# A codec kernel on one core: 16 rows per partition, tap sums in two buffers, PSUM by single banks, and a planner with new latencies and ranks that picks the engine of each residual update

## The chip, the cores and the metric

One core of one Trainium2 chip. The metric is the device time of one execution in microseconds (us). Most executions of a kernel agree within 0.3%.

Engines: TensorE (PE) multiplies matrices into PSUM; VectorE (DVE) and ScalarE (ACT) do elementwise work and read PSUM; GpSimd (POOL) does setup fills, edge copies and the issue of output stores. A "residual update" below is one correction of a block of 128 channels by a chosen codebook row.

## The reference, cut to what matters

```python
B, T, D, K = 2, 16000, 512, 3;  Nq, C = 4, 8          # bf16
xp = pad(x, 1)                                        # on the time axis
z = silu(sum(xp[:, i:i+T] * dw_enc[i] for i in range(K)))   # depthwise taps
res, q = z, 0
for s in range(Nq):                                   # four codebooks of 8 rows
    d2 = |res|^2 - 2 res.cb[s] + |cb[s]|^2
    sel = cb[s][argmin(d2)]
    q, res = q + sel, res - sel
y = sum(pad(q, 1)[:, i:i+T] * dw_dec[i] for i in range(K))
```

## The kernel before

The time axis is cut into tiles of `G` rows on each of 128 partitions (20 tiles of 6, 8 or 14 rows). Channels then lie on the partitions, by transposing loads. Per tile: three taps and their sum (DVE), exp and reciprocal (ACT), the gate product (DVE), scores of three codebooks at once (PE, read by DVE), a chain of some 25 tiny DVE instructions that decides three codebooks in turn, 24 residual updates, a fourth score and decision, and the output rows (PE, then ACT, then a store).

Nothing is issued in program order. Each instruction is a *step* with an estimated cost; a planner written in Python simulates the engines and emits the steps of each engine in the order in which it believes they become ready. That order is then fixed. What the planner believes of a step that depends on another is this:

```python
LATENCY = {"PE": 0.26, "ACT": 0.2, "DVE": 0.13, "POOL": 0.25, "SP": 0.1, "DMA": 0.05}
...
for u in users[n]:          # steps that depend on step n, which ends at t + c
    lat = self.LATENCY[s["e"]] if steps[u]["e"] != s["e"] else s["tail"]
    at[u] = max(at[u], t + c + (s["tail"] if steps[u]["e"] != s["e"] else 0.0) + lat)
```

A dependent step on *another* engine waits 0.13 to 0.26 us. A dependent step on the *same* engine is ready at once (`tail` is 0 for compute).

The tap sums and the residual updates:

```python
for c in range(2):                                    # two blocks of 128 channels
    for k, (dst, tok) in enumerate((p0[:, c], p1[:, c], P2[i % NP2])):   # cut
        add("DVE", ts, ..., tap(dst, i, k), ...)
        if k:
            tt(p0[:, c], p0[:, c], src, ALU.add, ...)
...
ON_DVE = (3, 7, 11, 15, 19, 23)                       # of the 24 updates of a tile
on_act = m not in ON_DVE
# ACT: two matmuls (identity * z + codebook), then a copy PSUM -> z
# DVE: one matmul (codebook), then z = z + PSUM
```

Of the kernel before, what the change touches and what calls it, by code (L numbers as in the profile page):

```python
# [16 lines left out]
class Plan:  # L17



    QUOTA = 2
    LATENCY = {"PE": 0.26, "ACT": 0.2, "DVE": 0.13, "POOL": 0.25, "SP": 0.1, "DMA": 0.05}

    def __init__(self, slots):
        self.steps, self.writer, self.readers = [], {}, {}
        self.slots = slots

    def add(self, engine, cost, key, fn, reads=(), writes=(), take=None, free=None, hold=None, tail=0.0, after=(), dest=None):
        n = len(self.steps)
        deps = set(after)  # L30
        for t in reads:
            if t in self.writer:
                deps.add(self.writer[t])
            self.readers.setdefault(t, []).append(n)
        for t in writes:
            if t in self.writer:
                deps.add(self.writer[t])
            deps.update(self.readers.get(t, ()))
            self.writer[t] = n
            self.readers[t] = []  # L40
        deps.discard(n)
        self.steps.append({"n": n, "e": engine, "c": cost, "k": key, "fn": fn, "deps": deps, "take": take, "free": free,
                           "hold": hold, "tail": tail, "dest": dest})
        return n

    def order(self):
        steps = self.steps
        left = [len(s["deps"]) for s in steps]
        users = [[] for _ in steps]
# [4 lines left out]
        clock = {s["e"]: 0.0 for s in steps}  # L54
        open_ = {e: [] for e in clock}
        table = [None]
        slots = {k: [0.0] * n for k, n in self.slots.items()}
        for s in steps:
            if not left[s["n"]]:
                open_[s["e"]].append(s["n"])  # L60
        out = []
        self.busy = {e: 0.0 for e in clock}
        held = {e: 0 for e in clock}

        def ready(n):
            s = steps[n]
            t = at[n]
            if s["take"]:
                if s["dest"] and held[s["dest"]] >= self.QUOTA:
                    return float("inf")  # L70
                t = max(t, min(slots[s["take"][0]]))
            return t

        while len(out) < len(steps):
            best = None
            for e, names in open_.items():
                now = clock[e]
                pick = None
                for n in names:
                    t = max(ready(n), now)  # L80
                    if t == float("inf"):
                        continue
                    r = (t, steps[n]["k"], n)
                    if pick is None or r < pick:
                        pick = r
                if pick and (best is None or pick < best):
                    best = pick
            t, _, n = best
            s = steps[n]
            c = s["c"]  # L90
            if s["hold"] and table[0] != s["hold"]:
                table[0] = s["hold"]
                c += 1.28
            if s["take"]:
                kind, box = s["take"]
                free = slots[kind]
                box["slot"] = free.index(min(free))
                box["kind"] = kind
                box["dest"] = s["dest"]
                if s["dest"]:  # L100
                    held[s["dest"]] += 1
                free[box["slot"]] = float("inf")
            s["t"] = t
            clock[s["e"]] = t + c
            self.busy[s["e"]] += c
            end = t + c + s["tail"]
            if s["free"]:
                if s["free"]["dest"]:
                    held[s["free"]["dest"]] -= 1
                slots[s["free"]["kind"]][s["free"]["slot"]] = end + self.LATENCY[s["e"]]  # L110
            open_[s["e"]].remove(n)
            out.append(s)
            for u in users[n]:
                lat = self.LATENCY[s["e"]] if steps[u]["e"] != s["e"] else s["tail"]
                at[u] = max(at[u], t + c + (s["tail"] if steps[u]["e"] != s["e"] else 0.0) + lat)
                left[u] -= 1
                if not left[u]:
                    open_[steps[u]["e"]].append(u)
# [5 lines left out]
def kernel(  # L124
# [15 lines left out]
    SIZES = ([6, 8] + [14] * 8, [14] * 8 + [8, 6])  # L140
# [6 lines left out]
    NX, NP, NP2, NZ, NOH, NY = 2, 3, 2, 3, 4, 3  # L147
    NA = 4
    ON_DVE = (3, 7, 11, 15, 19, 23)
# [29 lines left out]
    WDBC = sb([P, K, D], BF16, "WDBC")  # L179
# [11 lines left out]
    P2 = [sb([P, GM * P], BF16, f"P2{b}") for b in range(NP2)]  # L191
# [5 lines left out]
    YB = [sb([P, 8, D], BF16, f"YB{b}") for b in range(NY)]  # L197
# [15 lines left out]
    plan = Plan({"A": NA})  # L213
    add = plan.add

    def ps(box):
        return PS[box["slot"]]
# [7 lines left out]
    def mm(n):  # L225
        return max(0.06, 0.01 + n / 2400)

    wd_rows = bass.AP(tensor=dw_dec.tensor, offset=dw_dec.offset, ap=[[0, P], [D, K], [1, D]])
    add("ACT", 1.3, (-9,), lambda: nc.scalar.dma_start(out=WER, in_=dw_enc.rearrange("k (i p) -> (k i) p", p=P)), writes=["WER"], tail=3.0)
    add("ACT", 1.3, (-9,), lambda: nc.scalar.dma_start(out=CB1, in_=codebooks.flatten_outer_dims()), writes=["CB1"], tail=3.0)  # L230
# [3 lines left out]
    add("ACT", 1.3, (-8,), load_wd, writes=["WDBC"], tail=5.0)  # L234
    add("POOL", 3.0, (-9,), lambda: make_identity(nc, IDENT), writes=["I"])
# [4 lines left out]
    for b in range(NX):  # L240
        pool_memset(XT[b][:, :, 0, 0:2], 0.0, [("XE", b)], 0.3, (-8,))
# [4 lines left out]
    def setup():  # L246
        box = {}
        peb = lambda: ps(box).bitcast(BF16)[:, 0:K * KT]
        add("PE", 0.2, (-7,), lambda: nc.tensor.transpose(peb(), WER, IDENT[0:K * KT, 0:K * KT]), ["WER", "I"], [], take=("A", box))
        add("DVE", 0.15, (-7,), lambda: nc.vector.tensor_copy(WENC.rearrange("p k i -> p (k i)"), peb()), [], ["WENC"], free=box,  # L250
            after=[len(plan.steps) - 1])
        key = (0.9,)
        pool_memset(MSK, 0.0, ["MSK"], 0.8, (-6,))
# [3 lines left out]
        for b, t in enumerate(OHA):  # L257
            pool_memset(t, 0.0, [("OHA", b)], 0.8, (-5, b))
        for b, t in enumerate(OHW):
            pool_memset(t, 0.0, [("OHW", b, 0), ("OHW", b, 1)], 1.0, (-5, b))  # L260
        for b, t in enumerate(KEY):
            k16 = t.bitcast(U16).rearrange("p g (c h) -> p g c h", h=2)
            for c in range(C):
                pool_memset(k16[:, :, c, 0], c, [("KEY", b)], 0.2, (-4, b))
        for sk in CBN:
            pool_memset(CBN[sk], 0.0, [("CBN",) + sk], 0.5, (-3,))
        for i in range(KT):
# [3 lines left out]
                    ["CB1", "I"], [], take=("A", bx))  # L271
            j2 = add("ACT", 0.25, key, lambda i=i, p=ptb: nc.scalar.copy(CBT[:, i, :], p()), [], [("CBT", i)], after=[j])
            add("ACT", 0.25, key, lambda i=i, p=ptb: nc.scalar.mul(CBM2[:, i, :], p(), -2.0), [], [("CBM2", i)], free=bx, after=[j2])
        for b in range(NZ):
            for i in range(KT):
                eng = "ACT" if b == 0 else "DVE"
                f = nc.scalar.copy if b == 0 else nc.vector.tensor_copy
                add(eng, 0.4, (0.9 + b,), lambda b=b, i=i, f=f: f(ZB[b][:, i, :, 0:N3], CBM2[:, i:i + 1, 0:N3].to_broadcast([P, GM, N3])),
                    [("CBM2", i)], [("ZC", b)])
                add(eng, 0.25, (0.9 + b,), lambda b=b, i=i, f=f: f(ZB[b][:, i, :, N3 + P:ZW], CBM2[:, i:i + 1, N3:NC].to_broadcast([P, GM, C])),  # L280
                    [("CBM2", i)], [("ZC", b)])

        key = (0.95,)
        pool_memset(ONES, 1.0, ["ONES"], 0.3, (-5,))
# [5 lines left out]
        j = add("PE", 0.5, key, gramcb, [("CBT", i) for i in range(KT)], [], take=("A", bx))  # L290
# [16 lines left out]
        j = add("PE", 0.4, key, ccmm, ["CCD", "ONES"], [], take=("A", bc))  # L307
        j = add("ACT", 0.2, key, lambda: nc.scalar.copy(CCF[:, 0, :], ps(bc)[:, 0:NC]), [], ["CCF"], after=[j])
        j = add("ACT", 0.2, key, lambda: nc.scalar.copy(CCB[:, 0, :], ps(bc)[:, 0:NC]), [], ["CCB"], after=[j])
        pool_memset(CC2, 0.0, ["CC2"], 0.2, (-5,))  # L310
        add("ACT", 0.2, key, lambda: nc.scalar.copy(CC2[:, 0, 0:2 * C], ps(bc)[:, 0:2 * C]), [], ["CC2"], free=bc, after=[j])

        key = (1.0,)
# [3 lines left out]
        for s in range(2):  # L317
# [6 lines left out]
                    rhs=GP.rearrange("p q c -> p (q c)"), start=True, stop=True), [("SEL", s), "GP"], [], take=("A", bs))  # L324
            add("ACT", 0.25, key, lambda RP=RP, bs=bs: nc.scalar.mul(RP.rearrange("p q c -> p (q c)"), ps(bs)[0:GCM, 0:NPART * NC], 2.0),
                [], [("RP", s)], free=bs, after=[j])
            for s2 in range(s + 1, 3):
# [4 lines left out]
        key = (1.2,)  # L332
# [5 lines left out]
                stop=True), ["ROW", "CB1"], [], take=("A", br))  # L338
# [11 lines left out]
        key = (1.9,)  # L350
        WJ = [sb([P, D], BF16, f"WJ{j}") for j in range(2)]
        for v, tp in enumerate(((0, 1, 2, None), (None, 0, 1, 2), (None, None, 0, None), (None, 2, None, None))):
            acc = None
            for jj, k in enumerate(tp):
# [3 lines left out]
                add("ACT", 0.55, key, lambda t=t, k=k, jj=jj: nc.scalar.mul(t, WDBC[:, k, :], JM[jj]), ["WDBC", ("JM", jj)], [("WJ", jj % 2)])  # L358
# [3 lines left out]
            tt(WDEC[v], CB4, acc, ALU.mult, 0.35, key, ["CB4", ("WJ", aj)], [("WDEC", v)])  # L362

    def load(st):
# [6 lines left out]
        for g in range(G):  # L371
            add("SP", 1.35, (n - 2, g), lambda g=g: one(g), [], [("X", n % NX, g + 1)], tail=1.6)
        key = (n - 1.5,)
# [7 lines left out]
    def front(st, h):  # L381
# [6 lines left out]
        key = lambda f: (n + f,)  # L388
        allx = [("X", xs, g) for g in range(1, G + 2)] + [("XE", xs)]
        base = 0.45 * h  # L390
# [4 lines left out]
        for c in range(2):  # L395
            i = 2 * h + c
            ts = dve(R, 3.84) + 0.06
            for k, (dst, tok) in enumerate(((p0[:, c], ("P0", sl, c)), (p1[:, c], ("P1", sl, c)), (P2[i % NP2][:, 0:R], ("P2", i % NP2)))):
                add("DVE", ts, key(base + 0.01 * c), tap(dst, i, k), allx + ["WENC"], [tok])
                if k:  # L400
                    src = p1[:, c] if k == 1 else P2[i % NP2][:, 0:R]
                    tt(p0[:, c], p0[:, c], src, ALU.add, dve(R, 1.92), key(base + 0.01 * c), [tok], [("P0", sl, c)])
        add("ACT", act(2 * R), key(base + 0.05), lambda: nc.scalar.activation(p1, p0, ACT.Exp, scale=-1.0),  # L403
            [("P0", sl, 0), ("P0", sl, 1)], [("P1", sl, 0), ("P1", sl, 1), "ACTTAB"], hold="E")
        add("DVE", dve(2 * R, 3.84), key(base + 0.1), lambda: nc.vector.tensor_scalar(out=p1, in0=p1, scalar1=1.0, scalar2=None, op0=ALU.add),  # L405
# [3 lines left out]
    def front2(st, h, sl, p0, p1):  # L409
        n, G = st["n"], st["G"]  # L410
        R = G * P
        key = lambda f: (n + f,)
        base = 0.45 * h
        add("ACT", act(2 * R), key(base + 0.5), lambda: recip(p1, p1), [], [("P1", sl, 0), ("P1", sl, 1), "ACTTAB"], hold="R")
# [3 lines left out]
           key(base + 0.6), [("P0", sl, 0), ("P0", sl, 1), ("P1", sl, 0), ("P1", sl, 1)],  # L418
# [288 lines left out]
```

## Time and profile before

Median 872.5 us (870.7 to 876.0, 3 runs), later 874.2 of 4.

| | DVE | ACT | PE |
|---|---|---|---|
| busy us of the 872.9 us span | 784.2 (90%) | 678.7 (78%) | 625.1 (72%) |
| busy from 150 to 750 us | 573 of 600 | 498 | 460 |
| busy after 750 us (123 us) | 70 | 87 | 93 |

The page of the kernel before: busy time of each engine, and the busy share in tenths in 40 equal slices.

```profile
span 872.9 us, 12775 instructions
...
PE 625.1 (72%) x4685; PEld 371.6 (43%) x4739; DVE 784.2 (90%) x1518; ACT 678.7 (78%) x636; POOL 98.1 (11%) x193
...
DVE  8999999999999999899999999999999999986441
ACT  4544869796887879796988689869896899599752
```

DVE is at 90% or more from the second slice to the 35th, but for one; ACT has gaps throughout. The chain of waits, followed back from the last instruction (share of the span by engine, then by line):

```profile
DVE 69%; PE 18%; issue 9%; ACT 2%; DVEq 0%; DMA 0%; POOL 0%; POOLq 0%; ACTq 0%; SPq 0%
DVE P L393 12%; DVE P L244 11%; DVE ZB L580 11%; DVE ZB L244 5%; PE ps L572 5%; PE ps L571 4%; PE ps L437 4%; DVE rr L473 4%; DVE P L405 3%; DVE rr L596 3%; DVE KEY L244 2%; DVE V L244 2%; DVE OHA L244 2%; PE ps L630 2%; DVE M L502 2%
```

The groups of instructions on DVE (count, then busy us, mean ns of one, idle us before them): the tap sums, the taps, the residual updates.

```profile
L244 DVE TENSOR_TENSOR P<-P,P 128x1792 bf16<-128x1792 bf16 (+2 forms) x160 | 160.3, 1002 | 3.5
L393 DVE TENSOR_SCALAR P<-XT,WENC 128x1792 bf16<-128x1792 bf16 (+2 forms) x240 | 150.4, 648 | 0.7 <-issue 0.5
L580 DVE TENSOR_TENSOR ZB<-ZB,ps 128x896 bf16<-128x896 bf16 (+2 forms) x120 | 117.6, 988 | 27.1 <-PE ps L572 26.7
```

DVE's timeline before, in time order (start us, duration us, engine, line, operation).

```profile
424.04 0.28 DVE L244 TENSOR_TENSOR KEY<-V,CCB 128x112 bf16<-128x112 bf16 x1
424.36 0.27 DVE L502 TENSOR_REDUCE M<-KEY 128x14 f32<-128x112 f32 x1
424.66 0.28 DVE L244 TENSOR_TENSOR OHA<-KEY,M 128x112 bf16<-128x112 f32 x1
...
429.73 1.28 DVE L393 TENSOR_SCALAR P<-XT,WENC 128x1792 bf16<-128x1792 bf16 x2
430.92 0.95 DVE L596 TENSOR_REDUCE rr<-ps 128x6 bf16<-128x768 f32 x1
```

Of the first three, the second and the third read what the one before wrote: they start 0.03 to 0.04 us *after* the end of their predecessor. In the last two, the reduction has nothing to do with the taps before it, and starts 0.09 us *before* they end (429.73 + 1.28 = 431.01). All of this counts as "busy" or as gaps too small for a list.

### The profile page before, as it was taken

How to read it: one execution, taken by the hardware profiler on the slowest of the kernel's cores; microseconds unless marked ns; L12 is line 12 of the kernel's file. 1: busy time of each engine (PE TensorE's matmuls, PEld its weight loads, DVE VectorE, ACT ScalarE, POOL GpSimd, SP SyncE). 2: the span in 40 equal slices, each digit the busy share in tenths (PEclk: the TensorE clock that was granted, in tenths of full speed). 3: DMA queues.
4: the chain of work that ended last, by engine and by line, in shares of the span. 5: the costliest groups of instructions: out<-in, count | busy, mean ns of one | idle time of the engine just before them, and what ended most of it. 6: DMA issues, size and time to landing. Idle time of an engine off the chain costs nothing.

```text
span 872.9 us, 12775 instructions
## 1 busy us (share of the span) xinstructions
PE 625.1 (72%) x4685; PEld 371.6 (43%) x4739; DVE 784.2 (90%) x1518; ACT 678.7 (78%) x636; POOL 98.1 (11%) x193
## 2 busy tenths in 40 slices
PE   1054769595958686878787878877878787689973
PEld 0023335353535344444444544545445444345541
DVE  8999999999999999899999999999999999986441
ACT  4544869796887879796988689869896899599752
POOL 5000010110110101010110010102000111001101
PEclk9998589898898989798979997889899989999986
DMA  5430341426151716070815050516060412012212
GB/s 110 88 75 14 73 98 24 110 77 113 57 115 50 121 46 124 7 157 19 157 31 139 10 156 17 142 36 146 18 152 17 117 44 78 1 49 85 81 40 81
DMA packets 144231, 67.09 MB, mean 77 GB/s; under 512 B 139464, under 2 KB 139496, under 8 KB 141889
## 3 DMA queue, kind: packets, MB, share of 16 engines
q1 hardware_dynamic: 137088, 33.06, 19.7%
q0 software_dynamic: 6864, 32.77, 12.6%
q8 instruction: 37, 0.61, 0.3%
q10 hardware_dynamic: 216, 0.43, 0.2%
q14 instruction: 26, 0.21, 0.1%
HBM read 0.43 MB, written 32.77 MB: 38 GB/s over the span
## 4 chain that ended last, share of the span: by engine, by line
DVE 69%; PE 18%; issue 9%; ACT 2%; DVEq 0%; DMA 0%; POOL 0%; POOLq 0%; ACTq 0%; SPq 0%
DVE P L393 12%; DVE P L244 11%; DVE ZB L580 11%; DVE ZB L244 5%; PE ps L572 5%; PE ps L571 4%; PE ps L437 4%; DVE rr L473 4%; DVE P L405 3%; DVE rr L596 3%; DVE KEY L244 2%; DVE V L244 2%; DVE OHA L244 2%; PE ps L630 2%; DVE M L502 2%
## 5 line engine op out<-in xcount | busy, mean ns | idle before, releaser
L578 ACT CAST ZB<-ps 128x896 bf16<-128x896 f32 (+2 forms) x360 | 285.3, 870 | 40.8 <-PE ps L572 38.5
L572 PE MATMUL ps<-OHW,CBN 128*128 128x512 bf16 (+1 forms) x864 | 293.0, 373 | 13.7 <-DVE ZB L580 10.0
L571 PE MATMUL ps<-ZB,IDENT 128*128 128x512 bf16 (+1 forms) x648 | 242.8, 375 | 28.6 <-DVE ZB L580 17.2
L437 PE MATMUL ps<-ZB 128*128 128x136 bf16 (+1 forms) x2016 | 164.3, 232 | 36.6 <-DVE ZB L244 32.4
L638 ACT CAST YB<-ps 128x1024 bf16<-128x1024 f32 x126 | 130.5, 1046 | 70.2 <-PE ps L630 66.1
L437 PEld LDWEIGHTS <-ZB 128*128 128x128 bf16 x2016 | 144.8, 100 | 78.8 <-DVE ZB L244 34.3
L244 DVE TENSOR_TENSOR P<-P,P 128x1792 bf16<-128x1792 bf16 (+2 forms) x160 | 160.3, 1002 | 3.5
L403 ACT ACTIVATE P<-P 128x3584 bf16<-128x3584 bf16 (+2 forms) x40 | 116.2, 2906 | 46.1 <-DVE P L244 45.9
L393 DVE TENSOR_SCALAR P<-XT,WENC 128x1792 bf16<-128x1792 bf16 (+2 forms) x240 | 150.4, 648 | 0.7 <-issue 0.5
L572 PEld LDWEIGHTS <-CBN 128*128 128x128 bf16 x864 | 88.1, 102 | 139.4 <-issue 77.0
L580 DVE TENSOR_TENSOR ZB<-ZB,ps 128x896 bf16<-128x896 bf16 (+2 forms) x120 | 117.6, 988 | 27.1 <-PE ps L572 26.7
L423 ACT ACTIVATE P<-P 128x3584 bf16<-128x3584 bf16 (+2 forms) x40 | 114.9, 2892 | 12.1 <-DVE P L405 11.9
L661 POOL DMA_DIRECT2D out_dram<-YB x106 | 58.8, 560 | 445.0 <-ACT YB L638 423.9
L571 PEld LDWEIGHTS <-IDENT 128*128 128x128 bf16 x648 | 66.6, 103 | 76.3 <-issue 20.6
L434 PE MATMUL ps<-MSK,IDENT 128*128 128x408 bf16 (+3 forms) x180 | 62.3, 346 | 18.4 <-DVE S L474 8.3
L244 DVE TENSOR_TENSOR ZB<-P,P 128x3584 bf16<-128x3584 bf16 (+2 forms) x40 | 73.1, 1830 | 0.1
L630 PE MATMUL ps<-WDEC,OHW 128*128 128x512 bf16 x199 | 67.8, 412 | 5.9 <-DVE S L474 4.1
L545 PE MATMUL ps<-IDENT,OHA 128*32 128x128 bf16 x504 | 31.6, 282 | 35.5 <-DVE OHA L244 35.1
L596 DVE TENSOR_REDUCE rr<-ps 128x6 bf16<-128x768 f32 (+1 forms) x54 | 41.7, 771 | 9.5 <-PE ps L437 9.4
L473 DVE TENSOR_REDUCE rr<-ps 128x6 f32<-128x768 f32 (+1 forms) x54 | 41.7, 772 | 7.6 <-PE ps L437 7.5
L630 PEld LDWEIGHTS <-OHW 128*128 128x128 bf16 x252 | 25.6, 104 | 53.0 <-DVE OHW L549 22.3
L522 PE MATMUL ps<-BD,OT 112*128 112x112 bf16 (+2 forms) x180 | 17.0, 230 | 37.8 <-DVE OT L516 37.6
(92 smaller groups left out, 470.0 us busy)
## 6 DMA issues: line engine op xcount, KB each, us to landing
out_dram<-YB POOLq DMA_DIRECT2D x17, 896.0 KB, 5.6
out_dram<-YB POOLq DMA_DIRECT2D x18, 672.0 KB, 4.5
XT<-in_x_dram SPq DMA_TRANSPOSE x252, 2.9
out_dram<-YB POOLq DMA_DIRECT2D x14, 120.0 KB, 5.6
out_dram<-YB POOLq DMA_DIRECT2D x16, 90.0 KB, 4.4
out_dram<-YB POOLq DMA_DIRECT2D x1, 1024.0 KB, 5.8
WDBC<-in_dw_dec_dram ACTq DMA_DIRECT2D x1, 384.0 KB, 4.3
out_dram<-YB POOLq DMA_DIRECT2D x18, 6.0 KB, 1.9
```

The lines of the kernel that those rows point to most:

```text
L244: add("DVE", cost, key, lambda: nc.vector.tensor_tensor(out=out, in0=a, in1=b, op=op), reads, writes, **kw)
L393: return lambda: nc.vector.tensor_scalar(out=dst, in0=X[:, i, k:k + G, :].rearrange("p g c -> p (g c)"), scalar1=WENC[:, k, i:i + 1], scal ...
L403: add("ACT", act(2 * R), key(base + 0.05), lambda: nc.scalar.activation(p1, p0, ACT.Exp, scale=-1.0), [("P0", sl, 0), ("P0", sl, 1)], [("P ...
L423: nc.scalar.add_instruction(mybir.InstActivation(name=nc.get_next_instruction_name(), engine=mybir.EngineType.Activation, func=ACT.Reciprocal,
L437: nc.tensor.matmul(o[:, u * w:(u + 1) * w], lhsT=Z[:, i, b0 + u, N3:N3 + P], rhs=Z[:, i, b0 + u, c0:c1], start=False, stop=(u == nb - 1 an ...
L473: nc.vector.tensor_reduce(out=grp(rr[0], a, m)[:, :, :, 0], in_=v[:, :, :, N3:N3 + P], axis=AX.X, op=ALU.max)
L571: nc.tensor.matmul(o, lhsT=IDENT, rhs=zg[:, k0:k0 + nk, :], start=True, stop=False)
L572: nc.tensor.matmul(o, lhsT=CBN[s, u][:, i * P:(i + 1) * P], rhs=W[:, k0:k0 + nk, PADC:PADC + P], start=not on_act, stop=True)
L578: add("ACT", act(GH * P), key, lambda zg=zg, v=v: nc.scalar.copy(zg, v()), [], [tok], free=box, after=[j])
L580: add("DVE", dve(GH * P), key, lambda zg=zg, v=v: nc.vector.tensor_tensor(out=zg, in0=zg, in1=v(), op=ALU.add), [], [tok], free=box, after ...
L630: nc.tensor.matmul(o, lhsT=W[:, k, PADC:PADC + P], rhs=WDEC[u], start=True, stop=not wrap)
L638: add("ACT", act(1024), key, lambda k=k, box=box, Y=Y, k0=k0: nc.scalar.copy(Y[:, 2 * (k - k0):2 * (k - k0) + 2, :].rearrange("p g d -> p ...
```

## The change

Its intent: fewer, longer instructions (14 large tiles of 16 rows in place of 16 of 14), one buffer less and fewer adds in the tap sums, PSUM use in smaller pieces, and less residual work on DVE, chosen case by case. The planner's ranking of steps is written anew as a table, with other constants. The core of it (line numbers of the profile shift by about ten):

```diff
-    LATENCY = {"PE": 0.26, "ACT": 0.2, "DVE": 0.13, "POOL": 0.25, "SP": 0.1, "DMA": 0.05}
+    AGAIN = {"PE": 0.0, "ACT": 0.1, "DVE": 0.12, "POOL": 0.1, "SP": 0.0}
+    LATENCY = {"PE": 0.3, "ACT": 0.22, "DVE": 0.15, "POOL": 0.25, "SP": 0.1}
@@ order()
-                lat = self.LATENCY[s["e"]] if steps[u]["e"] != s["e"] else s["tail"]
-                at[u] = max(at[u], t + c + (s["tail"] if steps[u]["e"] != s["e"] else 0.0) + lat)
+                at[u] = max(at[u], t + c + self.AGAIN[e] if steps[u]["e"] == e else end + self.LATENCY[e])
@@ the engine of a residual update, picked when its matmuls are placed
+                if s["dest"] == "ANY":
+                    load = {d: max(clock[d] - t, 0.0) + held[d] + sum(steps[m]["c"] for m in waiting[d] if at[m] <= t + 1.0) for d in ("ACT", "DVE")}
+                    full = [d for d in load if held[d] >= self.QUOTA]
+                    box["dest"] = ("ACT" if full[0] == "DVE" else "DVE") if full else "DVE" if load["DVE"] + self.share < load["ACT"] else "ACT"
@@ kernel
-    SIZES = ([6, 8] + [14] * 8, [14] * 8 + [8, 6])
+    SIZES = ([6, 8] + [16] * 7, [16] * 7 + [8, 6])
-    ON_DVE = (3, 7, 11, 15, 19, 23)
+    SHARE = 4.78
+    WHEN = {"setup": (0, 0), "load": (-2, 1), "pad": (-1.5, 0), "taps": (0.049, 0.45), ...   # rank of each kind of step
@@ PSUM: "A" is a pair of banks, "S" a single bank, for the short transposes and small products
-            j = add("PE", 0.12, key(4.5), trans, [...], [], take=("A", box))
+            j = add("PE", 0.12, key(4.5), trans, [...], [], take=("S", box))
@@ tap sums
-        for c in range(2):
-            ... three taps in three buffers, an add of one block after the second and the third
+        for k in range(K):
+            for c in range(2):
+                add("DVE", ..., tap((p1 if k else p0)[:, c], 2 * h + c, k), ...)
+            if k:
+                tt(p0, p0, p1, ALU.add, dve(2 * R, 1.92), ...)          # both blocks at once
```

Cut: output buffers of four rows instead of eight (four of them), the decoder weights kept in one of them at the start, and GpSimd's first edge copies ordered ahead of its fills.

## The prediction

> **What bounds the kernel now.** VectorE (DVE). The page's busy table gives DVE 784.2 us of the 872.9 us span (90%), ScalarE (ACT) 678.7, TensorE (PE) 625.1. The chain of waits is 69% DVE, 18% PE, 2% ACT. Busy time by stretch: from 150 to 750 us DVE is busy 573 of 600 us (95.5%) and ACT 498 (83%); after 750 us DVE is busy only 69.6 of 123 us. So the middle is paid for in DVE work; the last 80 us are a chain across engines.
>
> **What the change does, costed from the trace** (counts from the order of instructions, durations from the groups by form):
> - Rows in all stay 252; tiles go from 20 to 18, large ones from 16 of 14 rows to 14 of 16. Only costs per instruction or per tile fall.
> - Residual updates on DVE: 120 become 73 (25% become 17%); ACT 360 become 359, but wider. DVE: 117.6 us for 96,768 elements a partition become about 84 us for 68,992 (1.08 us for 896 scales to 1.21 for 1024): -33 us. ACT: about +23 us; PE: about 10% more identity matmuls (242.8 us), +20 us.
> - Tap adds: 160 adds of one column block become 72 of two. An add of 1,792 starts a next one after 1.00 us, 0.93 of it data, and 0.1 later where it waits for the tap just before it. About -8 us. Taps: 24 fewer at some 0.15 us fixed: -4 us. The Trainium skill ("VectorE: DVE Perf Modes", the section on the fixed extra latency of SBUF-source operations) says many small operations pay it each time[...].
> - Small decision operations: about 32 a tile of 0.16 to 0.63 us, some 145 us on large tiles; two fewer such tiles, each operation 0.017 us longer: -12 us.
> - The 16th-row splits (6, 6, 4 instead of 6, 6, 2) need two views for the rest of 4: +4 us on DVE.
> - Exp and reciprocal table loads: 4 fewer at 1.28 us and 8 fewer activations: ACT -8 us.
>
> Sum: DVE about -55 to -65 us (to some 725), ACT to some 695, PE to some 630 to 645.
>
> **Critical path.** Nearly all of the DVE saving lies in the stretch where DVE is 95% busy, so it counts almost in full at first. But ACT rises, so DVE and ACT come within 5% of each other, and the waits between them grow: I give back some 5 to 10 us. Single PSUM banks for the short transposes free pairs for residuals and matter a little (DVE waits for PE residual matmuls only 26.7 us in all). First tap work starts earlier than 25 us, which helps ACT more than DVE. The tail stays about 80 us, with last tiles of 8 and 6 rows as before. Smaller stores (130 issues instead of 106) should fit: POOL is 11% busy.
>
> **Prediction.** 815 us, 8 in 10 between 795 and 838. Faster by over 2%: 0.95; within 2%: 0.04; slower: 0.01.
>
> **What would show each step.** DVE busy near 725, ACT near 695; residual adds on DVE near 84 us in the groups; tap adds near 2.2 us each; DVE about 92 to 95% and ACT about 90% busy in the middle stretches; chain of waits less DVE, more ACT and PE; first tap before 20 us.
>
> **What would make it wrong.** The fixed order not fitting real durations, so that DVE idles over 10% of the middle (slower than 838); output buffers of four rows making ACT wait for stores; POOL's setup work blocking DVE at the start, as it did for 9.4 us; or a plan that hides the tail, which would give under 795.

The cut passage misread the trace: it gave 0.37 us from start to start for taps of 768 elements, which is half of a merged row of two. In the trace before, one such tap starts 0.33 us after another, and one of 1,792 elements 0.60 us, so by my estimate from these two about 0.13 us does not grow with the elements.

## The result, and the profile after

Median 783.1 us (782.5 to 785.1, 4 runs) against 874.2: ratio 0.8966, 95% interval 0.893 to 0.900. A ratio here is the mean time of one kernel's runs over that of the other's of the same rounds, so it is not quite the ratio of the medians. Executions over 1.5% slower than the fastest of the same kernel are left out of the means. The kernel is faster, as forecast, but by 91 us where 59 were forecast, and outside the range.

The page of the changed kernel, the same parts as above.

```profile
span 780.5 us, 12263 instructions
...
PE 607.0 (78%) x4568; PEld 343.3 (44%) x4609; DVE 694.7 (89%) x1319; ACT 690.1 (88%) x623; POOL 146.9 (19%) x213
...
DVE  5999999999999999999999999999999987473541
ACT  3557869999999999999999999999999999959673
```

DVE lost 89.5 us of busy time, and its idle time stayed (span less busy time: 88.7 before, 85.8 after). ACT now is as full as DVE in the middle. The chain of waits after:

```profile
DVE 67%; PE 15%; ACT 9%; issue 7%; DMA 1%; DVEq 0%; POOL 0%; POOLq 0%; ACTq 0%
```

The same three DVE groups after:

```profile
L257 DVE TENSOR_TENSOR P<-P,P 128x4096 bf16<-128x4096 bf16 (+2 forms) x72 | 145.4, 2020 | 0.4
L405 DVE TENSOR_SCALAR P<-XT,WENC 128x2048 bf16<-128x2048 bf16 (+2 forms) x216 | 143.7, 688 | 0.3 <-issue 0.2
L588 DVE TENSOR_TENSOR ZB<-ZB,ps 128x1024 bf16<-128x1024 bf16 (+2 forms) x73 | 82.2, 1131 | 28.0 <-PE ps L580 23.2
```

Busy time by stretch, before and then after (columns: stretch, its length, busy us and instructions of PE, weight loads, DVE, ACT, POOL, then granted clock, DMA share, GB/s).

```profile
150.00:350.00 200.00, 146.19 (x1158) 89.55 (x1168) 191.34 (x352) 166.00 (x137) 23.06 (x38) 0.90 0.42 89
350.00:550.00 200.00, 158.47 (x1181) 95.33 (x1196) 190.68 (x330) 167.09 (x144) 19.29 (x33) 0.88 0.36 82
```

```profile
150.00:350.00 200.00, 164.75 (x1236) 94.05 (x1249) 198.90 (x334) 195.66 (x152) 43.24 (x42) 0.96 0.39 97
350.00:550.00 200.00, 173.50 (x1368) 99.56 (x1379) 197.90 (x349) 195.01 (x154) 31.46 (x47) 0.97 0.42 96
```

I had expected DVE and ACT to hinder each other as they come close in load. Instead DVE went from 95.5% to 99% busy there, and ACT from 83% to 98%. And DVE's timeline after, at the same decision steps:

```profile
412.47 0.17 DVE L492 CAST TR<-rr 128x16 bf16<-128x16 f32 x1
412.55 0.28 DVE L257 TENSOR_TENSOR PR<-S,CCF 128x128 bf16<-128x128 f32 x1
412.75 0.74 DVE L405 TENSOR_SCALAR P<-XT,WENC 128x2048 bf16<-128x2048 bf16 x1
413.42 0.28 DVE L257 TENSOR_TENSOR V<-PR,TR 128x128 bf16<-128x128 bf16 x1
413.62 0.74 DVE L405 TENSOR_SCALAR P<-XT,WENC 128x2048 bf16<-128x2048 bf16 x1
414.28 0.29 DVE L257 TENSOR_TENSOR KEY<-V,CCB 128x128 bf16<-128x128 bf16 x1
```

Between two links of the decision chain now stands a tap that has nothing to do with it. Every instruction starts 0.07 to 0.09 us before its predecessor ends. `V` takes 0.20 us from its start to the next start; in the kernel before a link took 0.30 to 0.32.

One can count this without a chip. In the program's DVE order I counted *dependent neighbours*: instructions that read a tile which the instruction just before them on DVE wrote. Before: 571 of 1514. After: 147 of 1315 (four memsets left out in both).

### The profile page after: what moved, and what is told of

The parts are those of the page before. It is cut to its first block, busy times and chain, and to the rows that moved or that the text cites. A ratio compares the mean times of both kernels' runs of the same rounds, so it can differ in the third digit from the quotient of the medians.

```text
span 780.5 us, 12263 instructions
## 1 busy us (share of the span) xinstructions
PE 607.0 (78%) x4568; PEld 343.3 (44%) x4609; DVE 694.7 (89%) x1319; ACT 690.1 (88%) x623; POOL 146.9 (19%) x213
## 4 chain that ended last, share of the span: by engine, by line
DVE 67%; PE 15%; ACT 9%; issue 7%; DMA 1%; DVEq 0%; POOL 0%; POOLq 0%; ACTq 0%
DVE P L405 13%; DVE P L257 11%; DVE ZB L588 8%; DVE ZB L257 7%; ACT ZB L586 4%; DVE rr L605 4%; DVE rr L480 4%; PE ps L579 4%; PE ps L580 4%; DVE P L414 4%; PE ps L444 3%; DVE OHW L556 2%; ACT YB L647 2%; DVE KEY L257 1%; DVE V L257 1%
## 5 line engine op out<-in xcount | busy, mean ns | idle before, releaser
L586 ACT CAST ZB<-ps 128x1024 bf16<-128x1024 f32 (+2 forms) x359 | 310.7, 986 | 40.5 <-PE ps L580 40.2
L444 PE MATMUL ps<-ZB 128*128 128x152 bf16 (+1 forms) x2016 | 160.6, 231 | 20.3 <-DVE ZB L257 13.2
L257 DVE TENSOR_TENSOR P<-P,P 128x4096 bf16<-128x4096 bf16 (+2 forms) x72 | 145.4, 2020 | 0.4
L405 DVE TENSOR_SCALAR P<-XT,WENC 128x2048 bf16<-128x2048 bf16 (+2 forms) x216 | 143.7, 688 | 0.3 <-issue 0.2
L412 ACT ACTIVATE P<-P 128x4096 bf16<-128x4096 bf16 (+2 forms) x36 | 116.6, 3243 | 15.5 <-DVE P L257 15.3
L430 ACT ACTIVATE P<-P 128x4096 bf16<-128x4096 bf16 (+2 forms) x36 | 113.3, 3187 | 0.2
L588 DVE TENSOR_TENSOR ZB<-ZB,ps 128x1024 bf16<-128x1024 bf16 (+2 forms) x73 | 82.2, 1131 | 28.0 <-PE ps L580 23.2
L257 DVE TENSOR_TENSOR ZB<-P,P 128x4096 bf16<-128x4096 bf16 (+2 forms) x36 | 72.5, 2014 | 0.0
L441 PE MATMUL ps<-MSK,IDENT 128*128 128x408 bf16 (+4 forms) x188 | 63.4, 337 | 7.1 <-ACT ZB L586 2.0
L390 POOL COPY XT<-XT 128x508 bf16<-128x508 bf16 x18 | 40.1, 2227 | 43.2 <-DVE P L405 18.8
L605 DVE TENSOR_REDUCE rr<-ps 128x6 bf16<-128x768 f32 (+3 forms) x62 | 42.7, 689 | 5.6 <-PE ps L444 5.6
L389 POOL COPY XT<-XT 128x508 bf16<-128x508 bf16 x18 | 17.1, 949 | 153.9 <-DMA XT<-in_x_dram 153.9
```

Source lines behind the costliest of these rows:

```text
L257: add("DVE", cost, key, lambda: nc.vector.tensor_tensor(out=out, in0=a, in1=b, op=op), reads, writes, **kw)
L405: return lambda: nc.vector.tensor_scalar(out=dst, in0=X[:, i, k:k + G, :].rearrange("p g c -> p (g c)"), scalar1=WENC[:, k, i:i + 1], scal ...
L412: add("ACT", act(2 * R), ("exp", n, h), lambda: nc.scalar.activation(p1, p0, ACT.Exp, scale=-1.0), [("P0", sl, 0), ("P0", sl, 1)], [("P1", ...
L430: nc.scalar.add_instruction(mybir.InstActivation(name=nc.get_next_instruction_name(), engine=mybir.EngineType.Activation, func=ACT.Reciprocal,
L444: nc.tensor.matmul(o[:, u * w:(u + 1) * w], lhsT=Z[:, i, b0 + u, N3:N3 + P], rhs=Z[:, i, b0 + u, c0:c1], start=False, stop=(u == nb - 1 an ...
L586: nc.scalar.copy(zg, v)
```

## The experiments

Theories. **A**: the time follows the DVE work that the structure of the change removes (fewer updates on DVE, fewer and longer instructions). **B**, the first rival: the gain came from order, constants and PSUM banks, which removed waits. From B grew **D**: the new wait between dependent steps of one engine (`AGAIN`) makes the planner put other work between dependent DVE instructions, which then overlap. Its rival **W**: the new ranking (`WHEN`) made the gain.

| run | what it is | median us | ratio to before | DVE busy us | dependent neighbours |
|---|---|---|---|---|---|
| before | | 872 to 875 | 1 | 784.2 | 571 |
| e4 | before + GpSimd's early edge copies | 877.7 | 1.0049 | 782.2 | – |
| e3 | before + 4 of 24 updates on DVE | 849.7 | 0.9727 | 741.7 | 551 |
| e11 | before + the wait | 830.7 | 0.9524 | 742.4 | 143 |
| e12 | before + the wait + 4 of 24 | 815.7 | 0.9353 | 716.5 | 262 |
| e15 | after, 14 rows, ranking searched for it | 798.9 | 0.9134 | 717.1 | 183 |
| after | | 783.1 | 0.8966 | 694.7 | 147 |
| e2 | after, adds split again | 785.9 | 0.9008 | 696.6 | – |
| e7 | after, PSUM in pairs | 781.2 | 0.8959 | 691.4 | – |
| e1 | after, every 4th update on DVE | 809.1 | 0.9276 | 721.7 | 137 |
| e5 | after, every 6th update on DVE | 802.8 | 0.9204 | 693.6 | 143 |
| e10 | e5 + old ranking | 820.2 | 0.9403 | 692.9 | 139 |
| e9 | e5 − the wait | 835.7 | 0.9566 | 724.4 | 489 |
| e6 | e5 + old ranking, old latencies, no wait | 862.7 | 0.9877 | 726.8 | 489 |
| e8 | e6 with 14 rows | 855.7 | 0.9811 | 736.2 | 539 |
| e13 | after + 432 independent tiny copies | 817.7 | 0.9375 | 732.1 | 147 |
| e14 | after + the same copies, dependent | 873.0 | 1.0001 | 769.9 | 543 |
| e16 | after, tuned on | 779.4 | 0.8911 | 695.2 | 124 |

All outputs were correct. "Dependent neighbours" marked – were not counted.

### e1, e5: which updates go to DVE

```diff
-  take=("A", box), dest="ANY"                                # the planner picks: 73 of 432 on DVE
+  on = "DVE" if m in (3, 7, 11, 15, 19, 23) else "ACT"       # e1: 108 of 432
+  on = "DVE" if m in (5, 11, 17, 23) else "ACT"              # e5: 72 of 432
```

> The changed kernel with the engine of each residual update fixed as before (every fourth of 24 on VectorE, 108 of 432) in place of the 73 that the plan picked; all else as changed. Theory A (time follows VectorE's own work in the middle): VectorE busy +34 us to about 729, ScalarE about -25 us, time about 805 to 820 us. Theory B (the gain came from the order, the latencies and the PSUM banks, which removed waits, not from less VectorE work): under 795 us.

> The changed kernel with the engine of each residual update fixed at every sixth (72 of 432 on VectorE), so the same share as the plan picked (73) but not its choice of which. Theory A (only the share counts): 780 to 788 us, VectorE busy about 694. Theory C (the plan's choice of which updates, made by how far each engine is behind, fills waits): 793 us or more at the same busy times, with more VectorE idle in the middle.

e1 came out at 809 us, just as theory A had it, with 33.8 us more in the update group and 27 us more DVE busy time (34 expected). That agreement misled me until e5: with the *same share* as the planner's pick (72 against 73) and the same DVE busy time (693.6 against 694.7) the time is still 802.8 us. So of the 26 us between e1 and the changed kernel only about 6 belong to the share, and 20 to the choice of which updates go where. The stretches of e5 show it as DVE idle time in the middle, 17 us of 400 where the changed kernel has 3:

```profile
150.00:350.00 200.00, 163.16 (x1186) 90.19 (x1185) 196.81 (x332) 191.69 (x147) 34.60 (x38) 0.94 0.39 91
350.00:550.00 200.00, 170.88 (x1351) 98.17 (x1350) 186.20 (x319) 193.99 (x152) 36.41 (x44) 0.97 0.41 98
```

Theory C of e5's expectation holds for this kernel and ranking.

### e2: the merged adds, in the same order

```diff
-                tt(p0, p0, p1, ALU.add, ...)                       # one add of two blocks
+                for c in range(2): nc.vector.tensor_tensor(out=p0[:, c], in0=p0[:, c], in1=p1[:, c], op=ALU.add)
```

> The changed kernel in exactly its order, but each two-block tap add is emitted as two one-block adds (72 adds become 144). Theory A: each further add costs 0.07 to 0.17 us of VectorE, so VectorE busy and time rise by 5 to 12 us (788 to 795 us). Theory B: no more than 3 us.

72 more adds cost 1.9 us of DVE busy time and 2.8 us of time, under what A expected: an independent add behind another overlaps with it. The two ratios' intervals overlap (0.8994 to 0.9022 here, 0.8930 to 0.9003 for the changed kernel), so merging the adds is worth about 3 us at most here.

### e3: the smaller share in the kernel before

```diff
-    ON_DVE = (3, 7, 11, 15, 19, 23)
+    ON_DVE = (5, 11, 17, 23)
```

> The kernel before with 4 instead of 6 of 24 residual updates on VectorE (80 of 480, the share of the changed kernel), nothing else. Theory A: VectorE busy -37 us, ScalarE +31 us, time about 840 to 850 us. Theory B: between 865 and 875 us, since the waits stay.

849.7 us: the share alone gives 22 us in the kernel before, at DVE busy −42 and ACT +31. A is right for this part.

### e4: the blocked copies at the start

```diff
-        key = (n - 1.5,)                       # GpSimd's edge copies of the tile
+        key = (n - 1.5 - 20 * (n == 0),)
```

> The kernel before with one edit: the two edge copies of the first tile on GpSimd are ordered ahead of its setup memsets, as in the changed kernel, so that GpSimd pauses for the load. If the 9.4 us in which three small VectorE copies sat at the start are time lost to the kernel, VectorE busy falls by about 9 us and the time by 4 to 9 us (865 to 870). If the block only moves behind the pause, or is hidden, the time stays within 2 us of 873.

In the kernel before, small DVE copies that come to 0.2 us each elsewhere sat for 9.4 us while GpSimd ran its fills. With the edit they run at once, but the fills are now later and block the first taps instead. First the kernel before, then e4:

```profile
1.53 9.42 DVE L319 COPY SEL<-IDENT 32x112 bf16<-32x112 bf16 x2
```

```profile
1.57 0.27 DVE L319 COPY SEL<-IDENT 32x112 bf16<-32x112 bf16 x2
...
11.49 4.82 DVE L393 TENSOR_SCALAR P<-XT,WENC 128x768 bf16<-128x768 bf16 x2 [1.21 <-POOL XT L376]
```

The first tap starts 13.5 us earlier (24.99 before), and the kernel is 0.5% *slower*. So an early start gained nothing in the kernel before; nothing suggests that the changed kernel's gain lies in its own (18.96 us), and the missing 9.4 us stall in its profile is no saving either: there two other copies sit for 6.07 us. The Trainium skill ("SBUF — State Buffer", section "Who interferes with whom") says that DVE copies in a two-port mode and GpSimd exclude each other for whole instructions. These traces agree that copies and taps stand still while fills run (9.42 and 4.82 us above); the mode they ran in is not shown.

### e7: pairs of PSUM banks again

```diff
-  take=("S", box)
+  take=("A", box)
```

> The changed kernel with every PSUM hand-out a pair of banks again (the four short users take a pair); the plan may pick anew. If single banks are worth little, as I predicted, 780 to 788 us; if they are a main part of the gain, 795 us or more.

781.2 us: the single banks are worth nothing measurable here (ratio 0.8959 against 0.8966; the planner picked anew).

### e6, e8: the old planner under the new structure

e6 takes e5 and gives the planner the old ranking (`WHEN` filled with the old keys), the old latencies and matmul rate, and no wait. e8 is e6 with 14 rows.

> As the fixed-sixth run, and besides with the old ranking of the steps and the old latencies in the plan (old matmul rate, no wait between dependent steps of one engine). Busy times should not change. If the new ranking and latencies are worth much (theory B), 10 us or more above the fixed-sixth run; if only the work per engine counts (theory A), within 4 us of it.

> As the run with fixed sixth and old ranking, with 14 rows a partition again (20 tiles, 80 of 480 updates on VectorE): the part of the 16 rows by itself. VectorE busy +12 to +20 us (two more tiles' decisions, 24 more taps, 8 more adds), ScalarE +10, time +12 to +22 us above that run.

This was the turning point. e6 has the 16 rows, the two-buffer taps, the single banks and the smaller DVE share, and takes 862.7 us: nearly the kernel before. Its instructions on DVE are those of e5, and their durations add up to the same within 5 us (783 against 779 us). But DVE is *busy* 33 us longer, against my expectation that "busy times should not change". First e5, then e6:

```profile
PE 622.6 (78%) x4617; PEld 346.5 (43%) x4617; DVE 693.6 (87%) x1318; ACT 695.5 (87%) x624; POOL 148.4 (19%) x213
PE 641.4 (74%) x4617; PEld 356.7 (41%) x4617; DVE 726.8 (84%) x1318; ACT 699.9 (81%) x624; POOL 136.7 (16%) x213
```

Busy time counts a moment once, however many instructions overlap in it. Same work and more busy time means less overlap. And e8, with smaller tiles, is 7 us *faster* than e6, where I had expected it 12 to 22 us slower: under the old order, 16 rows are worth nothing. Nor are the merged adds, the single banks and the smaller buffers: e8 has them, with the share of e3, and is 6 us slower than e3 (849.7 us).

### e9, e10: the wait or the ranking

```diff
-    AGAIN = {"PE": 0.0, "ACT": 0.1, "DVE": 0.12, "POOL": 0.1, "SP": 0.0}     # e9, from e5
+    AGAIN = {"PE": 0.0, "ACT": 0.0, "DVE": 0.0, "POOL": 0.0, "SP": 0.0}
```

e10 keeps the waits and takes only the old ranking.

> The fixed-sixth kernel (802.8 us) with one edit in the plan: a step may follow a dependent one on its own engine at once (the waits of 0.12 us on VectorE, 0.1 on ScalarE and GpSimd set to 0); ranking and other latencies as changed. Theory D (the wait makes the plan put other work between dependent VectorE instructions, which then overlap by about 0.1 us each): VectorE busy +20 to +35 us at the same instructions (about 715 to 728), time 820 to 850 us. Rival W (the new ranking made the gain): busy within 5 us of 694, time under 810 us.

> The fixed-sixth kernel with the old ranking of the steps only; the waits between dependent steps and the latencies as changed. Theory D: VectorE busy within 12 us of 694, time 800 to 825 us. Rival W: busy may stay, but waits come back: 835 us or more.

e9 has e5's instructions in another order and 33 us more time; the busy line shows where:

```profile
PE 628.7 (75%) x4617; PEld 351.1 (42%) x4617; DVE 724.4 (87%) x1318; ACT 696.0 (83%) x624; POOL 134.2 (16%) x213
```

DVE busy rose by 30.8 us for 346 more dependent neighbours (489 − 143): 0.09 us each. e10 leaves busy time and neighbours alone (692.9 us, 139) and costs 17 us, in idle time. So both count, by different means: the wait through overlap, the ranking through idle time.

### e11, e12: the wait alone, in the kernel before

```diff
-  lat = self.LATENCY[s["e"]] if steps[u]["e"] != s["e"] else s["tail"]
+  lat = self.LATENCY[s["e"]] if steps[u]["e"] != s["e"] else s["tail"] + {"ACT": 0.1, "DVE": 0.12, "POOL": 0.1}.get(s["e"], 0.0)
```

> The kernel before with one edit in its plan: a step that depends on one on its own engine is taken to be ready 0.12 us (VectorE) or 0.1 us (ScalarE, GpSimd) after it. Same instructions, another order. Theory D: VectorE busy falls by 20 to 35 us, time 835 to 858 us. Rival W: 868 us or more.

> The kernel before with that edit and with 4 of 24 residual updates on VectorE. If the two gains add (theory D): about 22 us under the run with the edit alone, 812 to 835 us. If ScalarE then limits, or the plan's fixed order breaks: 840 us or more.

One line in the planner, not one VectorE or ScalarE instruction more or less, and the kernel before falls from 872 to 830.7 us. DVE busy:

```profile
PE 626.5 (75%) x4739; PEld 369.4 (44%) x4739; DVE 742.4 (89%) x1518; ACT 676.0 (81%) x636; POOL 109.3 (13%) x193
```

That is −41.8 us at the same 1518 instructions, for 428 dependent neighbours fewer (0.10 us each), while DVE's idle time stayed (88.7 to 90.2 us). Both busy time and time fell by more than D expected (20 to 35 us, and 835 to 858 us). The decision chain now has a tap and a residual update between its links, as in the changed kernel:

```profile
437.75 0.67 DVE L393 TENSOR_SCALAR P<-XT,WENC 128x1792 bf16<-128x1792 bf16 x1
438.35 0.26 DVE L244 TENSOR_TENSOR V<-PR,TR 128x112 bf16<-128x112 bf16 x1
438.53 1.07 DVE L580 TENSOR_TENSOR ZB<-ZB,ps 128x896 bf16<-128x896 bf16 x1
439.53 0.27 DVE L244 TENSOR_TENSOR KEY<-V,CCB 128x112 bf16<-128x112 bf16 x1
```

Two rivals remain to be weighed. The edit also gives ScalarE and GpSimd a wait; ACT's busy time changed by only 2.7 us, but no run sets VectorE's wait alone. And the granted TensorE clock rises with the gains (0.892 in the profile before, 0.902 in that of e11, 0.956 after). Within e11 the faster runs had the higher clock (827.6 us at 0.923, 834.8 us at 0.902); which drives the other is not shown, but it is 7 us of 41. In e14 below, clocks from 0.902 to 0.948 go with times within 1.5 us, and what fell is VectorE's busy time.

With 4 of 24 updates as well (e12) it is 815.7 us: 15 us less again, where the share alone gave 22.

### e13, e14: the cost by itself

The changed kernel in its exact order, with twelve tiny copies after each of 36 DVE instructions, all reading a constant (e13), or each reading the one before it (e14):

```diff
             nc.vector.tensor_scalar(out=p1, in0=p1, scalar1=1.0, ...)
+            for j in range(12):
+                nc.vector.tensor_scalar(out=SCR[j], in0=CCF[:, 0, :], ...)                          # e13
+                nc.vector.tensor_scalar(out=SCR[j], in0=SCR[j - 1] if j else CCF[:, 0, :], ...)     # e14
```

> The changed kernel in exactly its order, with 12 tiny VectorE copies (32 fp32 columns each, a constant tile to scratch tiles that nobody reads) after each of the 36 plus-one instructions: 432 in all, none reads what another wrote. Theory D: about 0.08 to 0.12 us each from start to start, VectorE busy +35 to +52 us, time about +35 to +50 us.

> The same 432 tiny copies at the same places, but each reads the scratch tile that the one before it wrote (396 dependent neighbours more). Theory D: each dependent pair costs 0.09 to 0.13 us more than the independent one, so the time is 35 to 52 us above the independent probe. If dependence on the same engine costs nothing by itself, the two probes agree within 5 us.

One set of twelve in e13's timeline, then one in e14's:

```profile
300.96 1.11 DVE L418 TENSOR_SCALAR SCR<-CCF 128x32 f32<-128x32 f32 x12
```

```profile
306.58 0.17 DVE L418 TENSOR_SCALAR SCR<-CCF 128x32 f32<-128x32 f32 x1
306.79 2.35 DVE L418 TENSOR_SCALAR SCR<-SCR 128x32 f32<-128x32 f32 x11
```

Each takes 0.17 to 0.18 us. Independent, twelve fit in 1.11 us, so one starts 0.085 us after the other ((1.11 − 0.17) / 11). Dependent, eleven take 2.35 us: 0.217 us apart ((2.35 − 0.18) / 10). A dependence on the neighbour costs 0.13 us, and the kernel's time shows it in full: 817.7 to 873.0 us, 55 us for 396 pairs (0.14 each), a little over the 35 to 52 expected. The busy lines, e13 and then e14, show only a part of it:

```profile
PE 613.9 (75%) x4568; PEld 350.1 (43%) x4609; DVE 732.1 (90%) x1751; ACT 691.5 (85%) x623; POOL 148.4 (18%) x213
PE 624.1 (72%) x4568; PEld 360.9 (41%) x4609; DVE 769.9 (88%) x1751; ACT 694.3 (80%) x623; POOL 147.1 (17%) x213
```

DVE busy rises by 37.8 us, DVE idle by 17.4 us (84.2 to 101.6). So of the 0.13 us of a pair about 0.09 is lost overlap, which counts as busy, and about 0.04 is the gap before the dependent instruction, which does not. That fits the 0.09 to 0.10 us of busy time a pair in e9 and e11. In e11 the gaps of up to 0.06 us shrink too, from 20.4 us in all to 5.4, but other idle time took their place.

In the built programs nearly every dependent copy of e14 waits for the one before it on VectorE's own semaphore (396 of 432 copies have such a wait; 12 of e13's do), so the probes show a dependence together with the wait that enforces it. A wait for an older instruction costs nothing. Matching the traces with the programs: in e11, 552 VectorE instructions wait on that semaphore but do not read what the one in front wrote, and they start a median 0.078 us *before* its end; in the kernel before, 552 that do read it, and wait, start a median 0.034 us *after* its end. So what costs is to wait for the instruction just in front; whether the data or the wait does, no run separates.

### e15, e16: 14 rows with a ranking of its own, and an attempt at a better version

The changed kernel's ranking fits 16 rows: with 14 its planner runs into a dead end. So e15 has 14 rows and a ranking found by random search, with the planner's own estimate of the span as the score. e16 has 16 rows, last tiles of 10 and 4 rows and a ranking searched in the same way.

> The changed kernel with 14 rows a partition (20 tiles) and a ranking of the steps searched for these sizes; merged adds, single banks, the plan's pick and the waits between dependent steps stay. If the 16 rows carry a main part of the gain: 805 us or more. If the order carries it and the 16 rows only the fixed cost of two tiles (some 15 to 20 us of VectorE work, part of it hidden): 785 to 800 us.

> The changed kernel with last tiles of 10 and 4 rows instead of 8 and 6 and a ranking searched on for that: an attempt to better the result. VectorE and ScalarE are 97 to 99% busy in the middle, so only the first 60 and the last 130 us can give: 772 to 783 us, most likely within 1% of the changed kernel.

e15: 798.9 us, so most of the gain needs no 16 rows; they add about 16 us on top of a good order. The comparison is between two plans with rankings of their own, one of them from a random search, so this figure is softer than the others. e16: 779.4 us, ratio 0.8911 (0.8889 to 0.8933) where the changed kernel had 0.8966 (0.8930 to 0.9003) in another job; it is about half a per cent better, and the two intervals just overlap.

### The gain, step by step

From the runs above, each step on top of the one before (medians): the wait between dependent steps, 872 to 830.7 (−41); fewer updates on DVE, to 815.7 (−15); merged adds, single banks, the planner's pick and a ranking for it at 14 rows, to 798.9 (−17); 16 rows with their ranking, to 783.1 (−16). Another path would divide it otherwise: taken away one at a time from the changed kernel's side, the pick is worth 20 us, then the wait 33 or the ranking 17, and both together with the latencies 60.

## Why the prediction was wrong

The mechanism was right as far as it went: DVE bounds the kernel, and less DVE work is less time. A term of the sum was mis-sized, and a counter-term had the wrong sign.

| the prediction's step | forecast | measured |
|---|---|---|
| residual updates on DVE | −33 us | −35.4 (117.6 to 82.2) |
| tap adds | −8 | −14.9 (160.3 to 145.4); e2: about −3 of time at most from the merging itself |
| taps | −4 | −6.7 (150.4 to 143.7) |
| small decision operations | −12 | −14 by the sum of their durations; −33 by what each adds to the busy time, so 19 of it is overlap |
| DVE busy in all | −55 to −65, to some 725 | −89.5, to 694.7 |
| ACT busy | some 695 | 690.1 |
| PE busy | 630 to 645 | 607.0, at a granted clock of 0.956 instead of 0.892 |
| waits between DVE and ACT | +5 to +10 | DVE idle in all −2.9 (88.7 to 85.8) |
| single banks "matter a little" | | nothing measurable (e7) |
| tail as before, about 80 us | 0 | longer: DVE under 90% busy for the last 109 us before, for the last 156 us after |

**The step that failed** is the pricing of the DVE sum: "Only costs per instruction or per tile fall." I priced every instruction by its duration or by its count, and took the order as given. I had even measured the effect ("0.1 later where it waits for the tap just before it") and applied it to the tap adds alone, worth 8 us. It belonged to each of 571 dependent neighbours. The diff said so in plain sight: a new table with 0.12 us for VectorE. I read it as a better estimate of the planner's, not as a change of the kernel. The runs: −41 us of time and −42 of DVE busy from that line alone (e11), 33 and 31 us back when it is taken out (e9), 0.13 us a pair by itself (e14 against e13). The traces also show where it lies, when each moment of DVE busy time is counted to the instruction that extends it. The new order of e11 takes 31.4 us off the decision operations and 9.8 us off the tap adds, together 41.2 of its 41.8. In the changed kernel these two are 33.4 and 14.9 us less than before, where I had forecast 12 and 8; the updates, at −32 by this count, I had right.

**The second step that failed** is "I give back some 5 to 10 us". It treated the order as fixed while the loads come together. The new ranking and the pick place the work for those loads: without the pick 20 us come back at the same busy times (e5), without the ranking 17 more (e10). With the picks fixed the forecast waits do come, and more: DVE is idle for 108.0 us in e5, 19 more than before.

The prediction also said what would give under 795 us: a plan that hides the tail. That is not what happened; the tail became longer.

The sizes do not add up to a unique account of all 91 us, since the parts interact: the old ranking and latencies cost 60 us in e6, and the wait and the ranking undone singly cost 33 and 17 (the latencies between engines and the matmul rate, which e6 undoes too, no run undoes alone). What the 16 rows are worth depends on the order, too: 7 us the wrong way under the old one (e6, e8), about 16 the right way with rankings of their own (e15).

## What to carry to other kernels

A dependence on the instruction just before, on the same engine, is not free: 0.13 us here, beside 0.17 us for a tiny instruction itself, and some 0.09 of it is hidden in "busy". Count the dependent neighbours in the program's order, and try to put independent work between them, before making instructions fewer or larger (here −41 us, against −22 for fewer updates alone and nothing for 16 rows under the old order); where a scheduler orders the work, its table of latencies is part of the kernel. And read a busy time beside the sum of the durations: the same sum with more busy time is lost overlap. An undo-one run that lands where a theory said may do so for another reason (e1), so hold the share fixed and vary the choice (e5) as well.

## What the Trainium skill lacked or had wrong

- "VectorE: DVE Perf Modes", sections "The DRAIN you can't avoid" and "Rules for kernel authors": it says of chained VectorE instructions that the drain comes in any case, that a semaphore after each costs nothing extra, and that the count of instructions is what to reduce. Here a dependence on the instruction just before costs, together with its semaphore wait: dependent neighbours start 0.217 us apart, independent ones of the same form 0.085 us, and 396 such pairs cost 55 us. The first of the two sections also says that an instruction which is not held starts earlier; these traces agree with that (0.07 to 0.09 us before the end of the one in front). No page that I found gives what a dependence on the neighbour costs. In this kernel the order was worth more (e11, −41 us) than a lower count of updates on DVE (e3, −22 us).
- The same page, section on the fixed extra latency of SBUF-source operations (which my prediction rested on): it gives about 150 cycles of VectorE as the measured fixed term of one operation. In e13's rows of independent copies one copy lasts 0.17 us, but only 0.085 us pass from start to start: half of a copy is hidden by overlap. A single operation's fixed term thus overstates what a row of independent ones pays; the term's page does not say so, though other pages of the skill do reckon with overlap.
- "SBUF — State Buffer", section "Who interferes with whom": the exclusion of GpSimd and two-port VectorE copies holds per instruction there. In the trace before, three VectorE copies sat from 1.5 to 10.9 us, through a whole run of GpSimd fills of which none was longer than 0.9 us: back-to-back fills did not let VectorE in. In e4 two taps sat for 4.82 us, but got in while fills went on to 18.4 us, so it is not always the whole run. And freeing the copies gained nothing (e4, ratio 1.0049).
